# First unit's receptance and key products in fp32 with whole operands, their weights' parts made later, and another order at the start

## The chip, the cores and the metric

The kernel runs on one core of a Trainium2 chip. The metric is device time in microseconds; 660.84 us is the median of three runs before the change (660.57 to 663.16). Engines are named as the profile names them: PE (TensorE), DVE (VectorE), ACT (ScalarE), POOL (GpSimd), SP (the queue that issues the loads and stores).

## The reference

Banded attention over 8 batches, 8 heads and 576 positions of 64 columns (each position sees itself and the 63 before it), then an RWKV channel mix over the 512 joined columns:

```
attn = softmax(q k^T / 8 on the band);  x = (attn v), heads joined: [8, 576, 512]
x_prev = x shifted by one position, zeros first
xk = mu_k*x + (1-mu_k)*x_prev;   xr = mu_r*x + (1-mu_r)*x_prev
k = max(xk @ w_k, 0);   r = 1 / (1 + exp(-(xr @ w_r)))
out = r * ((k*k) @ w_v)
```

The three weights (512x1024, 1024x512, 512x512) arrive as 64-bit floats; q, k, v and mu as fp32.

## The kernel before, in words

The 4608 positions (8 batches of 576) are cut into nine units of 512 (`NU`, `TU`). A unit has four groups, one for each 128 of the 512 columns (two heads). Group by group, a *burst* on PE computes scores (16 fp32 matmuls of 64x128, `bank<-k,q`), transposes exponentials (8 fp32 transposes, `bank<-ident,pr`) and multiplies by the values (16, `bank<-pt,v`). The three parts of a burst belong to three groups that follow each other; only in the first groups they stand apart. DVE masks the scores and takes their least value (`least`, 8 pairs of rows for a group: `pr,nmax<-bank,mask`), ACT takes the exponentials, DVE the reciprocals of the sums, POOL or DVE scales. The result is copied to `xT`, with the column of the position before it.

`mix` then makes xr and xk: ACT or DVE a first term, DVE the blend (`d`). The blended operand is split in two fp32r parts that lie in one tile (`xs`): `high`, a cast on ACT, and `low`, the remainder on POOL or DVE.

A weight comes in chunks of 128x512, 20 in all: numbers 0 to 3 receptance, 4 to 11 key, 12 to 19 value. `decode` turns the 64-bit words into fp32: `sign` (ACT), `clamp` (DVE or POOL, `wt<-wt`), `shift`, `top` and `low` (DVE, the first two into a PSUM bank). `first_part` (a cast on ACT) and `second_part` (the remainder, POOL or DVE) then split the fp32 word into two fp32r parts, tile `ws`.

`product` multiplies: for every 128x128 weight piece three fp32r matmuls of 128x512 (high with high, high with low, low with high) add into one bank. In a unit there are 16 pieces for the receptance product (4 columns by 4 contraction steps), 32 for the key product and 32 for the value product. `r_units` makes the gate from the receptance bank: ACT a tanh and an exponential, DVE a minimum, an and-mask and the last product. `k_units` squares the rectified key and splits it (`ks`). `v_units` multiplies value banks by the gates and stores.

The order is not written down: each step is a `Piece` with a key, a cost and the engines that it may run on, and `play` lays the pieces out with a model of costs, of the rooms in each pool (8 PSUM banks, 14 large tiles `xs`) and of the port that DVE and POOL share. Keys set who goes first: `begin` for bursts, `DECODE` for chunks, `keys` for the mixes. Each engine then runs its pieces in that fixed order and waits where an operand is late. Almost every instruction is recorded by one helper, so the profile gives one line (L69 before, L79 after) for all of them, and tiles tell them apart.

Of the kernel before, what the change touches and what calls it, by code (L numbers as in the profile page):

```python
# [37 lines left out]

STEP = 6
# [3 lines left out]
JOINED = 6  # L43
LINK = 80
# [6 lines left out]
def attn_rwkv_kernel(ctx, tc, qT, kT, v2, mu_k, mu_r, w_k, w_v, w_r, out):  # L51
# [24 lines left out]
    class Hold:  # L76


        def __init__(self, tag):  # L79
            self.tag, self.users = tag, []  # L80

    class Piece:


        def __init__(self, engine, key, cost, fn, needs=(), takes=(), uses=(), lag=LINK, spare=0, port=False, size=0):
            self.costs = engine if isinstance(engine, dict) else {engine: cost}
            self.home = next(iter(self.costs))
            self.engine, self.key, self.fn = None, key, fn
            self.needs = [p for p in needs if p is not None]
            self.takes, self.uses, self.lag, self.spare, self.port, self.size = list(takes), list(uses), lag, spare, port, size  # L90
            for hold in (*self.takes, *self.uses):
                hold.users.append(self)
            self.done = None
            pieces.append(self)

    def play():
# [10 lines left out]
        times = [0]  # L107
        while any(left.values()):
            assert times, [(e, [(p.key, p.fn.__name__) for _, _, p in ps[:4]]) for e, ps in left.items()]
            now = heapq.heappop(times)  # L110
            while ends and ends[0][0] <= now:
                _, _, p = heapq.heappop(ends)
                for hold in (*p.takes, *p.uses):
                    users[id(hold)] -= 1
                    if not users[id(hold)]:
                        room[hold.tag] += 1
            for e, ps in left.items():
                if free[e] > now:
                    continue
                for _, n, p in ps:  # L120
                    if not all(q.done is not None and q.done + (q.lag if q.engine != e else 30) <= now for q in p.needs):
                        continue
                    tags = [h.tag for h in p.takes]
                    if any(room[tag] < tags.count(tag) + (p.spare if tag == "m" else 0) for tag in set(tags)):
# [8 lines left out]
                    for tag in tags:  # L133
                        room[tag] -= 1
# [22 lines left out]

    def pool_ns(n):
        return 195 + 2.1 * n

# [46 lines left out]
    def load_w(count):  # L207

        for n in range(len(raw), len(raw) + count):
            ws, w, i, c = chunks[n]  # L210

            def load(e, w=w, i=i, c=c, n=n):
                raw[n] = const.tile([P, WC, 2], U32, name="w", tag="w", bufs=len(chunks))
# [9 lines left out]
    words = {}  # L223

    def decode(n, loaded):
# [20 lines left out]
        def low(e):  # L246
            dve.scalar_tensor_tensor(words[n].bitcast(U32), raw[n][:, :, 0], 29, words[n, 0],
                                     op0=ALU.logical_shift_right, op1=ALU.bitwise_or)

        def first_part(e):  # L250
            ws[i, c] = const.tile([P, 2, WC], F32R, name="ws", tag="w", bufs=len(chunks))
            sca.copy(ws[i, c][:, 0], words[n])

        def second_part(e):
            engines[e].tensor_sub(ws[i, c][:, 1], words[n], ws[i, c][:, 0].bitcast(F32))

        p = Piece("ACT", key, 600, sign, [loaded], takes=[word])
        p = Piece({"DVE": 430, "POOL": 1000}, key, 0, clamp, [p], port=True)
        p = Piece("DVE", key, 700, shift, [p], takes=bits)
        p = Piece("DVE", key, 700, top, [p])  # L260
        p = Piece("DVE", key, 700, low, [p], uses=bits)
# [104 lines left out]
    def burst(key, gs=None, gt=None, gx=None, halves=(0, 1)):  # L366
        needs, takes, uses, cost, then = [], [], [], 100, []
        if gs is not None:
            needs.append(arrived[gs])
            uses += held[gs]  # L370
            cost += 1030
# [3 lines left out]
        if gx is not None:  # L375
            needs += [arrived["v", gx], *(chain.pop((gx, h, "kept")) for h in range(2))]
            uses += [*held["v", gx], *(chain.pop((gx, h, "pt")) for h in range(2))]
            cost += 1080
# [3 lines left out]
        if gt is not None:  # L382
            for h in halves:
                needs += chain.pop((gt, h, "scaled"))
                uses.append(chain.pop((gt, h, "pr")))
                cost += 355
# [95 lines left out]
    def mix(u, mu, mu1, c, key, after):  # L482
        g = u * NC + c
        state, scratch, x2, hold = [], Hold("tmp"), [], Hold("xs")
        by = []

        def diff(e):
            x2.append(act.tile([P, 2, TU], F32R, name="xs", tag="xs", bufs=SB))
            state.append(tmp.tile([P, TU], F32, name="d", tag="tmp", bufs=TB))
            by.append(e)  # L490
            if e == "ACT":
                sca.activation(state[0], xTs[g][:, :TU], AF.Copy, scale=mu1[:, c:c + 1])
            else:
                dve.tensor_sub(state[0], xTs[g][:, 1:], xTs[g][:, :TU])

        def blend(e):
            x, xp = xTs[g][:, 1:], xTs[g][:, :TU]
            if by[0] == "ACT":
# [13 lines left out]
        def high(e):  # L512
            sca.copy(x2[0][:, 0], state[0])

        def low(e):
            engines[e].tensor_sub(x2[0][:, 1], state[0], x2[0][:, 0].bitcast(F32))

        homes = {"ACT": act_ns(TU) + 90, "DVE": d1(TU)}
        p = after = Piece(homes if u < 2 else dict(reversed(homes.items())), key, 0, diff,
                          [*got[g], after, arrived["mu"]], [scratch, hold], port=True)  # L520
        p = Piece("DVE", key, d1(TU) + 30, blend, [p], uses=[held["x", g]], port=True)
        if 0 < -u * UB % NB < UB:
            p = Piece({"POOL": 200, "ACT": 190}, key, 0, seam, [p], uses=[held["x", g]])
        p = Piece("ACT", key, act_ns(TU), high, [p])
# [18 lines left out]
    def product(key, w, col, x, made, uses, count, n, spare=0):  # L543


        ps, held, last = [], [Hold("bank"), Hold("m")], opened[-1]
        for c in range(count):
            def fn(e, c=c):
                if c == 0:
                    ps.append(bank(TU))  # L550
                for a, b in ((0, 0), (0, 1), (1, 0)):
# [3 lines left out]
            needs = [last, *made[c], *decoded[id(w), c, col * P // WC]]  # L555
            last = Piece("PE", key + 3 * c / STEP, 3 * (13 + n / 2.4), fn, needs,
                         held if c == 0 else [], uses(c), lag=200, spare=spare if c == 0 else 0)
# [4 lines left out]
    def r_units(key, u, xr, gate, n=TU):  # L562
        made, hold = [x[2] for x in xr], [x[1] for x in xr]

        for m in range(NC):
            ps, held, p = product(key, wr_s, m, lambda c, e: xr[c][0][0][:, e], made, lambda c: [hold[c]], NC, n,
                                  spare=u > 0)
            state, scratch, result = [], Hold("tmp"), Hold("r")

            def powers(e, ps=ps, state=state):  # L570
                state += [tmp.tile([P, TU], F32, name="th", tag="tmp", bufs=TB),
                          tmp.tile([P, TU], F32, name="r", bufs=R_BUFS)]
                sca.activation(state[0], ps[0], AF.Tanh, scale=0.5)
                sca.activation(state[1], ps[0], AF.Exp)

            def share(e, state=state):
                th, r = state
                dve.tensor_scalar(r, r, 1.0, None, op0=ALU.min)
# [4 lines left out]
            p = Piece("ACT", key, 2 * act_ns(n), powers, [p], [scratch, result], held)  # L583
            p = Piece("DVE", key, 2 * d2(n) + d1(n), share, [p], uses=[scratch], port=True)
            gate.append((state, result, p))

    def k_units(key, u, xk, k2, n=TU):
        made, hold = [x[2] for x in xk], [x[1] for x in xk]
        for f in range(NF):
            ps, held, p = product(key, wk_s, f, lambda c, e: xk[c][0][0][:, e], made, lambda c: [hold[c]], NC, n,  # L590
                                  spare=u > 0)
            state, scratch, result = [], Hold("tmp"), Hold("xs")

            def relu(e, ps=ps, state=state):
                state.append(tmp.tile([P, TU], F32, name="kf", tag="tmp", bufs=TB))
                sca.activation(state[0], ps[0], AF.Relu)

# [6 lines left out]
            def high(e, state=state):  # L604
                state.append(act.tile([P, 2, TU], F32R, name="ks", tag="xs", bufs=SB))
                sca.copy(state[1][:, 0], state[0])
# [5 lines left out]
            p = Piece("ACT", key, act_ns(n), relu, [p], [scratch], held)  # L612
            p = Piece({"POOL": 150 + 1.8 * n, "ACT": act_ns(n)}, key, 0, square, [p])
            p0 = Piece("ACT", key, act_ns(n), high, [p], [result])
# [4 lines left out]
    def v_units(key, u, k2, gate, n=TU):  # L619
        for m in range(NC):  # L620
            ps, held, p = product(key, wv_s, m, lambda c, e: k2[c][0][1][:, e], [k[2] for k in k2],
                                  lambda c: [k2[c][1]], NF, n, spare=u > 0)
# [17 lines left out]
    DECODE = [-28 + 3 * n for n in range(4)] + [-14 + 2 * n for n in range(8)] + [2 + 2 * n for n in range(8)]  # L640
# [25 lines left out]
    def begin(k):  # L666
        return -30 + k if k < 4 else 10 * k - 60 if k >= JOINED + 2 else (-8, 0, 6, 12)[k - 4]
# [17 lines left out]

    last = None
    for u in range(NU):
# [3 lines left out]
        if u == 0:  # L691
            keys = {"xr": (-24, -23, -22, -21), "xk": (-19, -18, -17, -16)}
        else:
            keys = {"xr": [base - 40 + k for k in (25, 27, 29, 31)], "xk": [base - 40 + k for k in (33, 35, 37, 39)]}
        for nm, mu, mu1 in (("xr", mur, mur1), ("xk", muk, muk1)):
            xs[nm] = []
            for c in range(NC):
                xs[nm].append(mix(u, mu, mu1, c, keys[nm][c], last))
# [38 lines left out]
```

## Time and profile before

| what | value |
|---|---|
| median of three runs | 660.84 us |
| profiled execution: time, span | 662.79 us, 661.0 us |
| granted clock of PE over the span | 0.987 |
| first receptance product (TensorE) | 32.46 us |
| first key product | 58.11 us |
| first value product | 85.04 us |
| score matmuls of group 11 (start) | 143.73 us |

The last row serves as a common point: what lies behind it is the steady part, and both kernels reach it with the same products made. A product of one weight piece shows as three MATMUL rows when it is split. An fp32 matmul shows as two rows for one instruction: the 16 score matmuls of a group are 32 rows.

### The profile page before, as it was taken

To read this page: it belongs to the slowest core of one execution; us is meant where nothing else is said; L and a number is where in the kernel's file an instruction comes from. 1 tells how busy PE (TensorE), PEld (TensorE's weight loads), DVE (VectorE), ACT (ScalarE), POOL (GpSimd) and SP (SyncE) were. 2 spreads that over 40 slices of the span, in tenths; PEclk is the share of its full clock that TensorE was granted. 3 is DMA by queue.
4 is the path that set the end of the run, shared out by engine and by line. 5 is a ranking of instruction groups with operands and counts; after the bars stand their busy time and mean duration, and the time that the engine had idled before them with its cause. 6 is when DMAs were issued, how large, how long until landed. Compare 5 with 4: busy or idle time off the path is not lost.

```text
span 661.0 us, 12919 instructions
## 1 busy us (share of the span) xinstructions
PE 631.5 (96%) x4752; PEld 511.1 (77%) x4752; DVE 409.0 (62%) x1193; ACT 412.8 (62%) x1122; POOL 118.5 (18%) x186
## 2 busy tenths in 40 slices
PE   4875989999999999999999999999999999999997
PEld 4654768778888888888888888888888888888886
DVE  4899987795676467546755675558554766273311
ACT  6878695587754775477646864677367835671540
POOL 5468870110020012001200120001100110000000
PEclk9896999989999999999999999999999999999999
DMA  8991023522132113222332232223322210000001
GB/s 319 401 330 46 2 63 102 153 71 81 55 108 80 56 53 107 79 63 62 95 94 63 62 95 96 69 68 101 98 67 66 98 65 1 1 33 32 1 0 64
DMA packets 47583, 57.87 MB, mean 88 GB/s; under 512 B 7584, under 2 KB 39328, under 8 KB 47520
## 3 DMA queue, kind: packets, MB, share of 16 engines
q1 hardware_dynamic: 47520, 57.04, 26.7%
q8 instruction: 38, 0.62, 0.4%
q14 instruction: 25, 0.20, 0.1%
HBM read 47.58 MB, written 9.44 MB: 86 GB/s over the span
## 4 chain that ended last, share of the span: by engine, by line
PE 87%; DVE 5%; ACT 3%; issue 2%; DMA 1%; SPq 1%; POOL 0%; ACTq 0%; DVEq 0%; POOLq 0%
PE bank L69 87%; DVE bank L69 2%; DVE wt L69 1%; DMA qks<-qT 1%; ACT pr L69 1%; DVE r L69 1%; ACT d L69 1%; SPq L69 1%; ACT kf L69 0%; DVE pr L69 0%; DVE d L69 0%; ACT pt L69 0%; ACT ws L69 0%; ACT wt L69 0%; POOL xs L69 0%
## 5 line engine op out<-in xcount | busy, mean ns | idle before, releaser
L69 PE MATMUL bank<-xs,ws 128*128 128x512 f32 x1296 | 314.4, 398 | 7.1 <-DVE nmax L69 5.7
L69 PEld LDWEIGHTS bank<-xs,ws 128*128 128x128 f32 x1296 | 243.8, 190 | 64.7 <-issue 6.2
L69 PE MATMUL bank<-ks,ws 128*128 128x512 f32 x864 | 209.6, 396 | 1.2 <-ACT kf L69 1.2
L69 PEld LDWEIGHTS bank<-ks,ws 128*128 128x128 f32 x864 | 161.4, 188 | 38.5 <-ACT kf L69 1.9
L69 ACT ACTIVATE pr<-pr,nmax 128x128 f32<-128x128 f32 x288 | 111.8, 393 | 2.5 <-DVE nmax L69 2.3
L69 DVE TENSOR_TENSOR ks<-kf,ks 128x512 fp32r<-128x512 f32 x66 | 46.2, 701 | 83.0 <-ACT ks L69 82.9
L69 ACT ACTIVATE kf<-bank 128x512 f32<-128x512 f32 x72 | 43.0, 598 | 48.6 <-PE bank L69 47.0
L69 ACT COPY xT<-bank 128x512 f32<-128x512 f32 x34 | 20.0, 589 | 79.1 <-PE bank L69 79.0
L69 DVE CUSTOM_DVE_ANT_0 pr<-bank,maskNone 128x128 f32<-128x128 f32 x224 | 53.4, 285 | 14.9 <-PE bank L69 14.9
L69 DVE SCALAR_TENSOR_TENSOR r<-bank,r 128x512 f32<-128x512 f32 x36 | 24.9, 692 | 58.1 <-PE bank L69 58.0
L69 ACT ACTIVATE th<-bank 128x512 f32<-128x512 f32 x36 | 21.5, 598 | 62.7 <-PE bank L69 59.6
L69 POOL TENSOR_TENSOR kf<-kf 128x512 f32<-128x512 f32 x13 | 13.5, 1042 | 248.8 <-ACT kf L69 248.8
L69 ACT ACTIVATION_READ_ACCUMULATOR pr<-pr,nmax 128x1 f32 x288 | 55.1, 191 | 0.0
L69 PE MATMUL bank<-k,q 64*64 64x128 f32 x1088 | 40.8, 286 | 11.2 <-DMA q<-qT 6.5
L69 PEld LDWEIGHTS bank<-k,q 64*64 64x64 f32 x1088 | 31.7, 138 | 23.8 <-issue 9.1
L69 ACT CAST xs<-d 128x512 fp32r<-128x512 f32 x72 | 42.9, 616 | 6.5 <-DVE d L69 4.1
L69 ACT CAST ks<-kf 128x512 fp32r<-128x512 f32 x72 | 44.3, 617 | 1.8
L69 PE MATMUL bank<-ident,pr 128*128 128x128 f32 x288 | 43.1, 292 | 2.0 <-DVE pr L69 1.8
L69 PE MATMUL bank<-pt,v 128*64 128x64 f32 x1120 | 43.0, 229 | 2.0 <-ACT pt L69 2.0
L69 PEld LDWEIGHTS bank<-pt,v 128*64 128x64 f32 x1120 | 37.6, 141 | 9.0 <-issue 5.4
L69 POOL TENSOR_TENSOR xs<-d,xs 128x512 fp32r<-128x512 f32 x14 | 27.8, 1987 | 79.6 <-ACT xs L69 79.6
L69 POOL TENSOR_SCALAR pr<-pr,rs 128x128 f32<-128x128 f32 x68 | 28.5, 441 | 60.9 <-ACT d L69 50.2
(56 smaller groups left out, 580.3 us busy)
## 6 DMA issues: line engine op xcount, KB each, us to landing
v<-v SPq DMA_DIRECT2D x31, 192.0 KB, 2.9
w<-w_k SPq DMA_DIRECT2D x8, 512.0 KB, 8.3
w<-w_v SPq DMA_DIRECT2D x8, 512.0 KB, 10.7
v<-v SPq DMA_DIRECT2D x32, 128.0 KB, 2.4
v<-v SPq DMA_DIRECT2D x15, 256.0 KB, 3.5
v<-v SPq DMA_DIRECT2D x36, 64.0 KB, 2.5
w<-w_r SPq DMA_DIRECT2D x4, 512.0 KB, 5.7
outT<-r SPq DMA_DIRECT2D x8, 256.0 KB, 2.6
```

The source lines that it names most:

```text
L69: return lambda *args, **kw: tc.keep_in_program_order(op(*args, **kw))
```

## The change

- `direct` is true in unit 0 for receptance and key. There the operand is not split: `mix` writes the blend into one half of a shared tile (`xm`), `decode` writes the fp32 word into one half of a shared tile (`whole`), and `product` issues one fp32 matmul (`bank<-xm,whole`) in place of three. The value product and all later units are as before.
- The two parts of the receptance and key weights are still made, for unit 1, with keys of their own (`SPLIT`): chunks with higher numbers come first.
- More steps may run on more engines: the mix's first term and blend on POOL, the casts (`high`, `first_part`) on POOL.
- The gate of unit 0 (`GATES`): ACT takes abs, rectified negative, tanh and exponential (four instructions for two), DVE only the last product (one for three).
- `BEGIN`, `DECODE`, `MIX` and `MIX1` give new keys for the first groups, all chunks and the first two units' mixes. Some costs in the planner differ.

```diff
+GATES = 1
+DIRECT = "rk"
+SPLIT = (28, -13)
+BEGIN = (-31, -29, -29, -22, -9, -7, 14, 20)
+DECODE = (-35, -25, -1, -13, -17, -5, -4, -1, -10, 2, 11, 14, 12, 13, 15, 17, 22, 30, 26, 52)
 ...
         def low(e):
-            dve.scalar_tensor_tensor(words[n].bitcast(U32), raw[n][:, :, 0], 29, words[n, 0],
+            if plain:
+                if pairs[n // 2] is None:
+                    pairs[n // 2] = act.tile([P, 2, WC], F32, name="whole", tag="xs", bufs=SB)
+                words[n, 1] = pairs[n // 2][:, n % 2]
 ...
+        plain = direct(ws, 0)
 ...
+            whole[id(ws), i, c] = p, word, n
+            key = SPLIT[0] + SPLIT[1] * n
 ...
-        p0 = Piece("ACT", key, 560, first_part, [p])
+        p0 = Piece({"ACT": cast_ns(WC), "POOL": pool1_ns(WC)}, key, 0, first_part, [p], port=True)
 ...
+    def direct(ws, u):
+        return u == 0 and any(ws is a and nm in DIRECT for nm, a in (("r", wr_s), ("k", wk_s), ("v", wv_s)))
 ...
+                if plain:
+                    o = col * P % WC
+                    pe.matmul(ps[0], words[whole[id(w), c, col * P // WC][2], 1][:, o:o + P], x(c, None),
+                              start=c == 0, stop=c == count - 1)
+                    return
 ...
+                if u < GATES:
+                    sca.activation(state[0], ps[0], AF.Abs)
+                    sca.activation(state[1], ps[0], AF.Relu, scale=-1.0)
+                    sca.activation(state[0], state[0], AF.Tanh, scale=0.5)
+                    sca.activation(state[1], state[1], AF.Exp, scale=-1.0)
+                    return
```

On PE, around the receptance product and the start of the key product (`xs,ws` are split operand and weight parts, `xm,whole` the unsplit ones), the order was:

```order
L69 MATMUL bank<-pt,v 64x64 x16
L69 MATMUL bank<-ident,pr 128x128 x8
L69 MATMUL bank<-pt,vs 64x64 x16
L69 MATMUL bank<-xs,ws 128x512 x45
L69 MATMUL bank<-k,q 64x128 x16
L69 MATMUL bank<-xs,ws 128x512 x3
L69 MATMUL bank<-k,q 64x128 x16
```

and is now:

```order
L79 MATMUL bank<-pt,v 64x64 x16
L79 MATMUL bank<-xm,whole 128x512 x7
L79 MATMUL bank<-ident,pr 128x128 x4
L79 MATMUL bank<-xm,whole 128x512
L79 MATMUL bank<-ident,pr 128x128 x4
L79 MATMUL bank<-pt,vs 64x64 x16
L79 MATMUL bank<-xm,whole 128x512 x8
L79 MATMUL bank<-k,q 64x128 x16
L79 MATMUL bank<-xm,whole 128x512 x3
L79 MATMUL bank<-k,q 64x128 x16
```

Seven receptance products stand ahead of group 3's transposes and values; group 4's scores come after the whole receptance product, and three key products stand between them and group 5's scores.

On DVE, the key operand's blends of unit 0 (`d<-xT,muk`) stood among the decoding of key chunks, with their remainders behind them:

```order
L69 SCALAR_TENSOR_TENSOR d<-xT,muk,d 128x512
L69 TENSOR_SCALAR wt<-wt 128x512
L69 SCALAR_TENSOR_TENSOR d<-xT,muk,d 128x512
L69 TENSOR_SCALAR bank<-wt 128x512
L69 SCALAR_TENSOR_TENSOR bank<-w,bank 128x512
L69 SCALAR_TENSOR_TENSOR wt<-w,bank 128x512
L69 SCALAR_TENSOR_TENSOR d<-xT,muk,d 128x512
L69 TENSOR_TENSOR xs<-d,xs 128x512
```

They now stand behind six of the eight score rows of group 4 (two rows for each, the second `nmax`):

```order
L79 ISA pr,nmax<-bank,maskNone 128x128
L79 ISA nmax 128x1
L79 SCALAR_TENSOR_TENSOR xm<-xT,muk,xm 128x512
L79 SCALAR_TENSOR_TENSOR xm<-xT,muk,xm 128x512
L79 SCALAR_TENSOR_TENSOR xm<-xT,muk,xm 128x512
L79 SCALAR_TENSOR_TENSOR xm<-xT,muk,xm 128x512
L79 ISA pr,nmax<-bank,maskNone 128x128
```

All four key blends now come together, after group 4's scores, and no remainder follows them.

More of the change, by code (lines that the diff above doesn't have):

```diff
@@ L37 @@
 SB = 14
+GATES = 1
+DIRECT = "rk"
+SPLIT = (28, -13)
+WHOLE = 890
 STEP = 6
@@ L107, in play @@
         times = [0]
+        kept = len({id(h) for p in pieces if p.keeps for h in p.takes})
         while any(left.values()):
@@ L132, in play @@
                         left[o].remove((p.key, n, p))
-                    for tag in tags:
-                        room[tag] -= 1
+                    for hold in p.takes:
+                        if not hold.open:
+                            hold.open = True
+                            kept -= p.keeps
+                            room[hold.tag] -= 1
                     p.engine = e
@@ L250, in first_part @@
         def first_part(e):
-            ws[i, c] = const.tile([P, 2, WC], F32R, name="ws", tag="w", bufs=len(chunks))
-            sca.copy(ws[i, c][:, 0], words[n])
+            ws[i, c] = const.tile([P, 2, WC], F32R, name=f"ws{n}", tag=f"w{n}", bufs=1)
+            copy(e, ws[i, c][:, 0], words[n, 1])
         def second_part(e):
-            engines[e].tensor_sub(ws[i, c][:, 1], words[n], ws[i, c][:, 0].bitcast(F32))
-        p = Piece("ACT", key, 600, sign, [loaded], takes=[word])
-        p = Piece({"DVE": 430, "POOL": 1000}, key, 0, clamp, [p], port=True)
@@ L259, in decode @@
-        p = Piece("DVE", key, 700, shift, [p], takes=bits)
-        p = Piece("DVE", key, 700, top, [p])
-        p = Piece("DVE", key, 700, low, [p], uses=bits)
-        p0 = Piece("ACT", key, 560, first_part, [p])
+            engines[e].tensor_sub(ws[i, c][:, 1], words[n, 1], ws[i, c][:, 0].bitcast(F32))
+        plain = direct(ws, 0)
+        p = Piece("ACT", key, 670, sign, [loaded], takes=[word])
+        p = Piece({"DVE": 430, "POOL": 680}, key, 0, clamp, [p], port=True)
+        p = Piece("DVE", key, 700, shift, [p], takes=bits, uses=[word] if plain else [])
@@ new lines, in decode @@
+        p = Piece("DVE", key, 700, top, [p])
+        if plain:
+            if n % 2 == 0:
+                pairs[n // 2], rooms[n // 2] = None, Hold("xs")
+            word = rooms[n // 2]
+            p = Piece("DVE", key, 700, low, [p], takes=[word], uses=bits)
+            p.keeps = True
+            whole[id(ws), i, c] = p, word, n
+            key = SPLIT[0] + SPLIT[1] * n
+        else:
+            p = Piece("DVE", key, 700, low, [p], uses=bits)
+        p0 = Piece({"ACT": cast_ns(WC), "POOL": pool1_ns(WC)}, key, 0, first_part, [p], port=True)
@@ L366, in burst @@
     def burst(key, gs=None, gt=None, gx=None, halves=(0, 1)):
-        needs, takes, uses, cost, then = [], [], [], 100, []
+        needs, takes, uses, cost, then = [], [], [], 85, []
         if gs is not None:
@@ L370, in burst @@
             uses += held[gs]
-            cost += 1030
+            cost += 1034
             two = banks_of("s", "s")
@@ L385, in burst @@
                 uses.append(chain.pop((gt, h, "pr")))
-                cost += 355
+                cost += 424 if gx is not None else 355
                 own, = banks_of("t")
@@ L497, in blend @@
             x, xp = xTs[g][:, 1:], xTs[g][:, :TU]
-            if by[0] == "ACT":
+            if e == "POOL":
+                part = x2[0][:, 1].bitcast(F32)
+                pool.tensor_scalar(part, *((state[0], mu[:, c:c + 1]) if by[0] == "DVE" else (x, mu[:, c:c + 1])), 1.0,
+                                   op0=ALU.mult, op1=ALU.mult)
+                pool.tensor_add(state[0], xp if by[0] == "DVE" else state[0], part)
+            elif by[0] != "DVE":
                 dve.scalar_tensor_tensor(state[0], x, mu[:, c:c + 1], state[0], op0=ALU.mult, op1=ALU.add)
@@ L541, in attn_rwkv_kernel, with product @@
     opened = [None]
-    def product(key, w, col, x, made, uses, count, n, spare=0):
+    def product(key, w, col, x, made, uses, count, n, spare=0, u=1):
         ps, held, last = [], [Hold("bank"), Hold("m")], opened[-1]
+        plain = direct(w, u)
         for c in range(count):
```

129 lines of the change are left out of this document (90 added, 39 removed).

## The prediction

> **What bounds the kernel now.** I read the page's totals and slices first, then a table of busy time by stretches, then who waited for whom, then TensorE's timeline where the table shows a hole.
>
> ```profile
> span 661.0 us, 12919 instructions
> PE 631.5 (96%) x4752; PEld 511.1 (77%) x4752; DVE 409.0 (62%) x1193; ACT 412.8 (62%) x1122; POOL 118.5 (18%) x186
> PE   4875989999999999999999999999999999999997
> ```
>
> One slice is 16.5 us. PE is full from the tenth slice on; what it lacks lies in the first nine. I cut the span where PE's work changes kind (PE, PEld, DVE, ACT, POOL busy, granted clock):
>
> ```profile
> 0.00:32.46 32.46, 21.82 (x288) 17.68 (x288) 20.65 (x94) 23.87 (x84) 15.76 (x48) 0.95 0.96 359
> 32.46:46.14 13.68, 13.19 (x82) 9.54 (x80) 12.89 (x18) 9.92 (x18) 8.77 (x7) 1.00 0.97 356
> 46.14:58.11 11.97, 2.12 (x32) 1.51 (x33) 11.94 (x42) 10.91 (x34) 8.67 (x8) 0.72 0.45 132
> 58.11:103.60 45.49, 42.74 (x293) 33.73 (x294) 42.36 (x99) 35.95 (x83) 33.21 (x39) 0.96 0.08 24
> 103.60:143.73 40.13, 38.15 (x333) 30.53 (x331) 30.30 (x102) 26.91 (x95) 5.29 (x10) 0.96 0.43 129
> 143.73:640.00 496.27, 496.27 (x3657) 404.55 (x3657) 288.07 (x839) 305.24 (x812) 46.78 (x74) 1.00 0.21 65
> ```
>
> From 143.73 us PE never idles, with DVE busy 58% and ACT 62% (288.07 and 305.24 of 496.27). So the end follows from one number: when PE reaches that point with the work ahead of it done. The worst stretch is the third, where PE works 2.12 of 11.97 us and DVE 11.94.
>
> ```profile
> PE bank L69 <- DVE nmax L69: 5.7, 1, 5.7
> PE bank L69 <- DVE wt L69: 5.2, 3, 4.1
> ```
> ```profile
> 50.77 1.70 PE L69 MATMUL bank<-k,q 64*64 64x128 f32 x30 [4.06 <-DVE wt L69]
> 58.11 1.62 PE L69 MATMUL bank<-xs,ws 128*128 128x512 f32 x3 [5.65 <-DVE nmax L69]
> 60.24 1.54 PE L69 MATMUL bank<-xs,ws 128*128 128x512 f32 x3
> 61.97 15.68 PE L69 MATMUL bank<-xs,ws 128*128 128x512 f32 x66
> ```
>
> The receptance product of the first unit is done at 46.14; the key product begins at 58.11. Between them stands DVE: decoding weights (wt) and the softmax of groups 4 and 5 (nmax). The stage is bound by DVE's queue, not by PE or the loads.
>
> **The change, part by part.** *The dearer product.* One product of a 128x128 weight piece was three fp32r matmuls; for 16 receptance and 32 key pieces of unit 0 it becomes one fp32 matmul, which the trace does not show at this size.
>
> ```profile
> 92.09 8.62 PE L69 MATMUL bank<-ks,ws 128*128 128x512 f32 x36
> 100.64 1.10 PE L69 MATMUL bank<-k,q 64*64 64x128 f32 x32
> 101.67 1.15 PE L69 MATMUL bank<-pt,v 128*64 128x64 f32 x32
> 102.75 1.09 PE L69 MATMUL bank<-ident,pr 128*128 128x128 f32 x8
> 103.60 7.93 PE L69 MATMUL bank<-ks,ws 128*128 128x512 f32 x33
> 634.02 0.85 PE L69 MATMUL bank<-xs,ws 128*128 128x512 f32 x3
> 634.72 0.87 PE L69 MATMUL bank<-ks,ws 128*128 128x512 f32 x3
> ```
>
> Start to start, three fp32r matmuls take 634.72 - 634.02 = 0.70 us. The nearest fp32 rows: four transposes (8 records, full 128x128, 128 columns) take 103.60 - 102.75 = 0.85, or 0.213 per 128 columns, so 0.85 for 512. The score matmuls (four quadrants at a time, 128 columns) take 1.03/4 = 0.26, so 1.03. I take 0.88, near the transposes, which fill the array as the new product does; the bounds are 0.85 and 1.03. The 48 products then cost 48 x (0.88 - 0.70) = +8.6 us of PE, bounds +7.2 and +15.8.
>
> The Trainium skill (FP8 and Floating Point Precision, section TensorE Precision Notes) speaks against the change: true fp32 takes four passes through the array. Priced at a third of a triple each, 0.233, that is an estimate of 0.93 and +11.0 us, between the bounds above.
>
> *The start.* Before, a first operand went blend, cast, remainder on POOL; the last step alone:
>
> ```profile
> 26.57 0.75 DVE L69 SCALAR_TENSOR_TENSOR d<-xT,mur,d 128x512 f32<-128x512 f32 x1 [0.20 <-ACT d L69]
> 28.19 1.81 POOL L69 TENSOR_TENSOR xs<-d,xs 128x512 fp32r<-128x512 f32 x1 [2.67 <-ACT xs L69]
> 28.69 1.97 PE L69 MATMUL bank<-ident,pr 128*128 128x128 f32 x8
> 32.46 3.29 PE L69 MATMUL bank<-xs,ws 128*128 128x512 f32 x13
> ```
>
> Now the blend (27.3) is enough, and the transposes and values of group 3 (28.69 to 32.46) come after seven products. The first product can start near 28.8 instead of 32.46. The second weight chunk and blend must be there soon after, and DVE now splits the first weight chunk between the softmax of groups 0 and 1, some 0.7 us and a wait for ACT's cast, with group 1's score rows queued behind it; I allow 27 to 31. Then 16 x 0.88 = 14.1, group 3's transposes 0.85 and values 1.08: receptance done at 44.8, group 4's scores at 45.8. The 3.7 us won at the start are spent on dearer products: before, it was 46.14.
>
> *The hole.* The first key product waits for DVE's queue. In the changed order DVE has ahead of it 38 score rows, 26 decode instructions (9 shifts, 9 tops, 8 lows), 7 clamps, 6 blends, 3 copies, 4 pairs of share instructions, 1 split and 2 small ones. Durations:
>
> ```profile
> 33.33 0.69 DVE L69 TENSOR_SCALAR bank<-wt 128x512 uint32<-128x512 uint32 x1
> 34.05 0.70 DVE L69 SCALAR_TENSOR_TENSOR bank<-w,bank 128x512 uint32<-128x512 uint32 x1
> 34.79 0.69 DVE L69 SCALAR_TENSOR_TENSOR wt<-w,bank 128x512 uint32<-128x512 uint32 x1
> 51.05 0.28 DVE L69 CUSTOM_DVE_ANT_0 pr<-bank,mask 128x128 f32<-128x128 f32 x1
> 51.26 0.28 DVE L69 CUSTOM_DVE_ANT_0 pr<-bank,maskNone 128x128 f32<-128x128 f32 x1
> 27.84 0.42 DVE L69 TENSOR_SCALAR wt<-wt 128x512 f32<-128x512 f32 x1
> 24.55 0.68 DVE L69 COPY pt<-bank 128x512 f32<-128x512 f32 x1
> 22.07 0.16 DVE L69 TENSOR_SCALAR rs<-sums 128x8 f32<-128x8 f32 x1
> 22.27 0.20 DVE L69 RECIPROCAL rs<-rs 128x8 f32<-128x8 f32 x1
> ```
>
> 38 x 0.21 (start to start) = 8.0; 26 x 0.69 = 17.9; 7 x 0.42 = 2.9; 6 x 0.75 = 4.5; 3 x 0.68 = 2.0; 4 x 0.36 = 1.4; 0.7 + 0.5; in all 37.9 us. Before, DVE had worked 20.65 + 12.89 + 11.94 = 45.5 us by 58.11. What is gone from the queue is group 5's scores, one to two chunks, two key blends and two operand remainders. DVE cannot start before the first scores (6.32), and by 32.46 it had idled 32.46 - 6.32 - 20.65 = 5.5 us for its inputs. With the same idle, 6.3 + 5.5 + 37.9 = 49.7. The other path, group 4's scores at 45.8 plus six score rows and two blends (1.3 + 1.5), gives 48.6. I take 50.5, since DVE's instructions stretch while POOL works:
>
> ```profile
> 40.42 1.76 POOL L69 TENSOR_TENSOR ws<-wt,ws 128x512 fp32r<-128x512 f32 x1
> 40.94 1.53 DVE L69 TENSOR_SCALAR wt<-wt 128x512 f32<-128x512 f32 x1
> 42.38 1.78 DVE L69 SCALAR_TENSOR_TENSOR d<-xT,muk,d 128x512 f32<-128x512 f32 x1
> ```
>
> A clamp of 0.42 took 1.53 and a blend of 0.75 took 1.78 beside POOL's remainders. POOL still makes the parts of the weights in this time, so this stays; bounds for the key product's start are 48.6 and 54.
>
> A hole of about 3 us also costs less behind it: after the old one the first triple took 60.24 - 58.11 less two transposes (0.7), or 1.4 us instead of 0.70, at a granted clock of 0.72. The Trainium skill (TensorE: Matmul & The Clock Gate, section What's actually happening) has the clock halve after an idle window of about 3.4 us; by that rule a 3 us hole may keep it, and the trace agrees as far as it goes: the half-speed triple stands behind a wait of 5.65 us.
>
> *Key product to the common point.* From 50.5: 32 x 0.88 = 28.2; group 5's scores 1.0; group 4's transposes 0.85; bursts 6 and 7 at 103.60 - 100.64 = 2.96 each, 5.9; six value-product records 1.4: 37.4, so 87.9. The decode of the last key chunk has 19.8 us more of DVE queue ahead (16 decode instructions, 10 score rows, 4 gates, 2 blends, copies): ready at 70.3, needed about 72. That is what comes late next; I allow 2 us: 89.9. Before, the same work was done at 103.60 less 39 records of (100.64 - 92.09)/36 = 0.2375, or 94.3. Gain there 4.4.
>
> From there to the start of burst 11:
>
> ```profile
> 133.15 1.02 PE L69 MATMUL bank<-ident,pr 128*128 128x128 f32 x4 [1.84 <-DVE pr L69]
> 143.73 1.10 PE L69 MATMUL bank<-k,q 64*64 64x128 f32 x32
> ```
>
> Before: 143.73 - 94.3 = 49.4. Full speed: 150 records x 0.2375 = 35.6 and three bursts 8.9, 44.5. The stall at 133.15 came from bursts 9 and 10 standing nine records apart; the order now has 36 and more between bursts. I allow 1.1 us: 45.6, so 89.9 + 45.6 = 135.5 against 143.73: -8.2 us.
>
> *What costs nothing.* The parts of key and receptance weights, made later, take 12 casts and 12 remainders; they are hidden behind the fp32 products, but the first split products of unit 1 need them, over 20 us later. The value weights' last parts have 29.6 us of DVE queue behind 70.3, so 100; needed near 113 for the last eighth of the value product. The gates of unit 0 lose two DVE instructions each and gain two on ACT (4 x 2 x 0.6 us); ACT idles in every stretch shown. In later units POOL takes 26 mixes and 21 casts: it worked 46.78 of 496.27 us there. Uncovered, each would add about a microsecond, once per operand. The loads' order on SP is unchanged but for one pair of stores; nothing waits for those.
>
> The sum stands on the profiled execution: 661.0 - 8.2 = 652.8 us span. That run took 662.79 us; the runs' median is 660.84, 1.95 below. Against the median I predict 660.84 - 8.2, **652.6 us**.
>
> **The rivals.** *All cover holds*: no late chunk, products at 0.85, start at 27. That takes off the 2 and 1.1 us allowed and 32 x 0.03 = 1.0: -12.3, and with the key start at 48.6 -14.2: 647. For it: by the queue sums the last key chunk (70.3 against 72) and the value parts (100 against 113) are in time. Against it: no early stretch of the trace is free of stalls.
>
> *The win is eaten*: key product at 54 and the value product waiting some 4 us for parts, since POOL and DVE exclude each other as at 40.42. That adds 3.5 + 4 to -8.2: 660.
>
> *Slower: the hole stays.* Key banks come free only when ACT has read the receptance banks, and ACT's queue now holds four instructions per gate with group 4's eight exponentials between them, which wait for DVE. If DVE is as late as before, the key product starts at 58.1 again; with 37.4 + 2 it ends its stage at 97.5 against 94.3, and with the later stalls as before: +3.2, 664; with products at 1.03 another 4.8, 669. It turns slower once the key product starts later than 58.7 at my price, or 50.5 + 3.4 at 1.03. For it: DVE was 11.94 of 11.97 us busy there. Against it: 7.6 us have left its queue.
>
> **How the numbers follow.** Forecast 0.55, full cover 0.17, win eaten 0.15, hole stays 0.13. Below 0.5% (3.3 us, about what a measurement can tell from no change) lie the forecast, full cover and a fifth of the third: faster 0.75; same 0.12; slower 0.13. The range, 645 to 661.5, takes in full cover and the win eaten, and leaves out the slow case and a little below.
>
> **What would show it.** In the changed profile: 48 products of about 0.88 us; the first before 31 us, the key product at 49 to 52, PE full from about 52 with gaps of 2 us in all; burst 11 near 135.5; the rest as now, about 517 us. It is wrong if a product is over 1 us, if DVE still shows a hole over 6 us before the key product, or if PE idles in the value product or after 140.

## The result, and the profile after

The changed kernel takes 652.44 us (median, 651.96 to 653.41) against 660.75 us for the kernel before on the same chip: a ratio of 0.987, with a 95% interval of 0.985 to 0.989, or 8.3 us less. The profiled execution took 653.41 us with a span of 651.6; the one before took 662.79 with a span of 661.0. That pair differs by 9.4 us.

The page's totals and TensorE's slices (16.3 us each) of the kernel after:

```profile
span 651.6 us, 12842 instructions
...
PE 632.5 (97%) x4704; PEld 497.0 (76%) x4704; DVE 399.6 (61%) x1174; ACT 389.4 (60%) x1076; POOL 144.5 (22%) x250
...
PE   4879999999999999999999999999999999999997
```

From the fourth slice on TensorE's digit is now 9; before, that was so from the seventh, with stalls up to 133 us. PE's busy time hardly moved (631.5 to 632.5): the dearer products fill time in which it waited or ran slowly. POOL has taken 26 us more (118.5 to 144.5), DVE and ACT 33 less together.

The table by stretches of the kernel after, cut at the same times as before up to 143.73 (busy time of PE, PEld, DVE, ACT, POOL, then granted clock, DMA share and GB/s):

```profile
0.00:32.46 32.46, 20.86 (x259) 14.43 (x260) 21.78 (x96) 24.54 (x85) 19.26 (x56) 1.00 0.94 346
32.46:46.14 13.68, 12.76 (x94) 6.67 (x92) 12.61 (x25) 11.32 (x21) 10.55 (x16) 1.00 0.94 350
46.14:58.11 11.97, 9.12 (x44) 4.21 (x45) 8.78 (x40) 8.71 (x33) 5.61 (x11) 0.71 0.47 151
58.11:103.60 45.49, 45.49 (x333) 28.77 (x332) 42.86 (x110) 39.33 (x109) 34.93 (x50) 1.00 0.25 72
103.60:143.73 40.13, 40.13 (x349) 32.63 (x348) 30.22 (x93) 24.29 (x79) 10.34 (x12) 1.00 0.31 95
```

The third stretch was the hole: PE worked 2.12 of 11.97 us there and now works 9.12, though at a granted clock of 0.71. In the two stretches after it PE no longer idles at all (42.74 and 38.15 busy before, now 45.49 and 40.13). TensorE's timeline shows what is left of the hole (start, busy time, what, idle time before it and what ended it):

```profile
27.71 6.27 PE L79 MATMUL bank<-xm,whole 128*128 128x512 f32 x14
...
37.47 7.13 PE L79 MATMUL bank<-xm,whole 128*128 128x512 f32 x16
44.53 1.10 PE L79 MATMUL bank<-k,q 64*64 64x128 f32 x32
48.99 5.46 PE L79 MATMUL bank<-xm,whole 128*128 128x512 f32 x6 [3.36 <-ACT pr L79]
54.38 1.42 PE L79 MATMUL bank<-k,q 64*64 64x128 f32 x32
...
61.00 8.75 PE L79 MATMUL bank<-xm,whole 128*128 128x512 f32 x20
69.68 1.10 PE L79 MATMUL bank<-k,q 64*64 64x128 f32 x32
...
88.87 6.82 PE L79 MATMUL bank<-ks,ws 128*128 128x512 f32 x27
...
137.92 1.10 PE L79 MATMUL bank<-k,q 64*64 64x128 f32 x32
```

An unsplit product is two rows, so `x6` is three products. They take 54.38 - 48.99 = 5.39 us; ten later ones take 69.68 - 61.00 = 8.68, or 0.868 each. So the three products behind the hole ran at half speed. After 48.99 no row of PE up to burst 11 has a wait.

Burst 11 starts at 137.92, but this is not quite the same point as 143.73 before, although the table of the time before calls it a common point: the 96 split records of unit 0's value product stand ahead of it in both orders, but of unit 1 there are 78 now and were 63, so 15 more (of 0.2375 us each). With the same work done, the common point is 137.92 - 15 x 0.2375 = 134.4, so 9.4 us earlier. Behind it lie 517.2 us (before 517.3): all of the profiled pair's gain is made ahead of this point.

| milestone | before | predicted | after |
|---|---|---|---|
| first receptance product | 32.46 | 28.8 | 27.71 |
| first key product | 58.11 | 50.5 | 48.99 |
| key product, bursts 6 and 7 and six value records done | 94.3 | 89.9 | 88.87 |
| common point | 143.73 | 135.5 | 134.4 |
| median | 660.84 | 652.6 | 652.44 |

### The profile page after: what moved, and what is told of

It reads as the page before. It is cut to its first block, busy times and chain, and to the rows that moved or that the text cites. A ratio compares the mean times of both kernels' runs of the same rounds, so it can differ in the third digit from the quotient of the medians.

```text
span 651.6 us, 12842 instructions
## 1 busy us (share of the span) xinstructions
PE 632.5 (97%) x4704; PEld 497.0 (76%) x4704; DVE 399.6 (61%) x1174; ACT 389.4 (60%) x1076; POOL 144.5 (22%) x250
## 4 chain that ended last, share of the span: by engine, by line
PE 94%; ACT 2%; DVE 0%; issue 0%
PE bank L79 94%; ACT pr L79 1%; ACT th L79 0%; ACT pt L79 0%; ACT r L79 0%; ACT xT L79 0%; DVE r L79 0%; ACT xm L79 0%
## 5 line engine op out<-in xcount | busy, mean ns | idle before, releaser
L79 PE MATMUL bank<-xs,ws 128*128 128x512 f32 x1152 | 275.6, 396 | 0.0
L79 PEld LDWEIGHTS bank<-xs,ws 128*128 128x128 f32 x1152 | 215.8, 188 | 49.4
L79 DVE TENSOR_TENSOR ks<-kf,ks 128x512 fp32r<-128x512 f32 x69 | 48.2, 699 | 83.1 <-ACT ks L79 82.5
L79 PE MATMUL bank<-xm,whole 128*128 128x512 f32 x96 | 46.0, 626 | 3.4 <-ACT pr L79 3.4
L79 DVE TENSOR_TENSOR xs<-d,xs 128x512 fp32r<-128x512 f32 x59 | 38.3, 684 | 8.4 <-POOL xs L79 5.6
L79 POOL TENSOR_SCALAR pr<-pr,rs 128x128 f32<-128x128 f32 x88 | 35.4, 424 | 31.0 <-ACT d L79 17.0
L79 PE MATMUL bank<-pt,v 128*64 128x64 f32 x1120 | 41.0, 225 | 1.0 <-ACT pt L79 1.0
L79 PEld LDWEIGHTS bank<-pt,v 128*64 128x64 f32 x1120 | 35.9, 138 | 7.7 <-issue 5.5
L79 ACT CAST xs<-d 128x512 fp32r<-128x512 f32 x57 | 35.4, 620 | 8.6 <-DVE d L79 6.9
```

The source lines that it names most:

```text
L79: return lambda *args, **kw: tc.keep_in_program_order(op(*args, **kw))
```

## The experiments

The first four sections undo one part of the change each. Every run was timed beside runs of the kernel before, whose medians lie between 661.1 and 661.4; the ratio is against those. Only the three runs on the finished order, at the end, leave everything else in its place. In all others the planner lays out the whole start anew, so what such a run measures is its edit together with the order that the planner then makes.

### All products split again

The planner's lists, the choice of engines and the gates stay as after; the diff is in one constant:

```diff
-DIRECT = "rk"
+DIRECT = ""
```

> All products of unit 0 are split again (three fp32r matmuls); the new keys, the flexible engines and the four-instruction gate stay. Theory A (the unsplit products pay by shortening what stands ahead of the key product on DVE, POOL and ACT, and cost 48 x 0.175 = 8.4 us of PE): the key product starts at 54 to 60 us, PE saves 8.4 us later, and the time is 656 to 662 us. Theory B (the new order and the flexible engines bring the gain, the unsplit products only cost PE time): the key product still starts near 49 us and the time falls to 644 to 649 us.

Measured: 666.95 us (666.14 to 668.02), ratio 1.008 [1.006, 1.010]. Neither number: it is slower than the kernel before. TensorE's timeline of this run:

```profile
43.61 0.80 PE L79 MATMUL bank<-xs,ws 128*128 128x512 f32 x1 [2.58 <-POOL ws L79]
...
58.36 2.90 PE L79 MATMUL bank<-ident,pr 128*128 128x128 f32 x8 [5.42 <-POOL pr L79]
60.92 3.28 PE L79 MATMUL bank<-xs,ws 128*128 128x512 f32 x7
```

With split products the early work waits for remainders from POOL (2.58 us within the receptance product), and the hole comes back ahead of group 4's transposes (5.42, booked to POOL's scaling). Against the kernel after, whose lists, engines and gates are the same, unsplit products are worth 666.95 - 652.44 = 14.5 us, although each of the 48 costs PE more. The lists were made for unsplit products; which list would suit split ones best was not tried.

### The old lists

`BEGIN`, `DECODE`, `MIX` and `MIX1` as before (16 receptance and 32 key products stay unsplit, engines and gates stay new):

```diff
-BEGIN = (-31, -29, -29, -22, -9, -7, 14, 20)
+BEGIN = (-30, -29, -28, -27, -8, 0, 6, 12)
-DECODE = (-35, -25, -1, -13, ...)
+DECODE = (-28, -25, -22, -19, ...)
-MIX = ((-51, -31, -47, -56), (-43, -46, -33, -40))
+MIX = ((-24, -23, -22, -21), (-19, -18, -17, -16))
 ...
```

> The keys of before (for the first groups, the chunks and the mixes of units 0 and 1) with the unsplit products kept. Theory A: most of the gain stays, 652 to 657 us, the key product starts before 54 us. Theory B: the gain goes and the dearer products remain, 660 to 669 us.

Measured: 662.44 us (659.63 to 662.95), ratio 1.001 [1.000, 1.002]: B's number, no gain over the kernel before. Its timeline:

```profile
36.77 1.46 PE L79 MATMUL bank<-pt,vs 128*64 128x64 f32 x30 [1.28 <-ACT pt L79]
...
75.11 16.46 PE L79 MATMUL bank<-xm,whole 128*128 128x512 f32 x34 [2.40 <-ACT kf L79]
```

The rest of the change, unsplit products included, brings nothing by itself: the key product does start early, at 51.10, but the waits are only spread out, down to 75.11. The change without the unsplit products (the run above) costs 6 us. Together the two gain 8.3. With these lists, each is good only with the other.

### Only one of the two products unsplit

```diff
-DIRECT = "rk"
+DIRECT = "r"     (the other run: "k")
```

> Only the receptance product is unsplit, the key product is split again. Theory A: PE saves 32 x 0.175 = 5.6 us, but the key parts come before the key product again, so it starts at 53 to 58 us: 653 to 659 us. Theory B: the saving remains, 646 to 649 us.

Measured: 663.17 us (661.32 to 664.94), ratio 1.002 [1.001, 1.004]. The hole of this run, and the one where the key product alone is unsplit, each from TensorE's timeline:

```profile
56.68 1.52 PE L79 MATMUL bank<-ident,pr 128*128 128x128 f32 x4 [7.30 <-POOL pr L79]
```

```profile
51.22 2.10 PE L79 MATMUL bank<-k,q 64*64 64x128 f32 x30 [3.01 <-DVE nmax L79]
```

The key product started at 57.86, as late as before the change, and that is where A had put it (53 to 58); the time is beyond both numbers, since further waits followed (2.24 us at 90.89 for the value operand, 1.41 and 1.65 in unit 1's receptance product).

> The kernel after with the receptance products of the first unit split into parts again and only its key products unsplit; lists of positions and engine choice as after. It completes the square of no unsplit product (666.95), receptance alone (663.17) and both (652.44). If the two halves add up: 666.95 - (663.17 - 652.44) = 656.2, so 655 to 658 us. If the new order needs both (a late receptance stage pushes the rest as in the run with all split, key product not before 53 us): 660 to 665 us.

Measured: 658.32 us (657.09 to 659.79), ratio 0.995 [0.994, 0.997], just above the first number. None 666.95, receptance alone 663.17, key alone 658.32, both 652.44: the halves add up within 2.1 us (3.8 and 8.6 alone, 14.5 together). So neither half needs the other; most of it is the key product's.

### The old choice of engines

POOL may no longer take first terms, blends and casts:

```diff
-        p0 = Piece({"ACT": cast_ns(WC), "POOL": pool1_ns(WC)}, key, 0, first_part, [p], port=True)
+        p0 = Piece("ACT", key, cast_ns(WC), first_part, [p])
-        homes = {"ACT": cast_ns(TU) + 110, "POOL": pool1_ns(TU), "DVE": d1(TU)}
+        homes = {"ACT": cast_ns(TU) + 110, "DVE": d1(TU)}
 ...
```

> The casts run on ACT alone and the mixes' first terms and blends not on POOL, as before; unsplit products and new keys stay. Theory A: 651 to 655 us, since ACT idles in each early stretch and PE is full later. Theory B: 655 to 660 us, since POOL's help is part of what brings the gain. In both the stretch behind 140 us stays at full PE.

Measured: 656.23 us (654.77 to 659.21), ratio 0.992 [0.990, 0.995], by the median B's number. TensorE's timeline has one large wait:

```profile
40.72 5.40 PE L79 MATMUL bank<-xm,whole 128*128 128x512 f32 x8 [4.29 <-DVE xm L79]
```

The last receptance operand then comes 4.29 us late from DVE. POOL's help is worth 3.8 us, by medians, of the gain; the runs spread widely, and the profiled execution (654.93) is only 1.5 us behind that of the kernel after.

### One list at a time

The kernel after with the old `DECODE` alone, then with the old `BEGIN` alone (the diffs are those lines of the run with the old lists).

> The kernel after with the old order of weight decoding alone (the old list of decoding positions; the new positions of the units' starts, the unsplit products and the engine choice stay). If the decoding order carries the gain of the order (the last receptance and key chunks then come late on DVE, and TensorE waits for them): 657 to 663 us, near the 662.4 us with all old lists. If the positions of the units' starts carry it: 652 to 655 us.

> The kernel after with the old positions of the units' starts alone (groups 2 and 3 then begin ahead of the receptance product; the new decoding order, the unsplit products and the engine choice stay). If these positions carry the gain of the order: 657 to 663 us, with the receptance product done near 51 us. If the decoding order carries it: 652 to 655 us.

Measured: 659.38 us (657.57 to 660.43), ratio 0.997 [0.996, 0.998], and 660.85 us (657.03 to 663.33), ratio 1.000 [0.998, 1.002]. Neither list carries the gain alone: each one put back takes nearly all of it. The key product starts at 49.68 and at 52.38, so an early key product alone is not the gain; PE must also have no wait before and behind it. The largest late wait of each, in their timelines:

```profile
74.01 13.98 PE L79 MATMUL bank<-xm,whole 128*128 128x512 f32 x28 [2.54 <-ACT xT L79]
```

```profile
52.38 3.28 PE L79 MATMUL bank<-xm,whole 128*128 128x512 f32 x4 [1.76 <-DVE nmax L79]
```

### Two tries at the hole through the planner

The hole of 3.36 us is where DVE's four key blends stand behind six score rows of group 4:

```profile
46.96 3.22 DVE L79 SCALAR_TENSOR_TENSOR xm<-xT,muk,xm 128x512 f32<-128x512 f32 x4
```

The row is from DVE's timeline of the kernel after. By the durations of the four (one of 1.23 us, three of 0.74) the second ends at 46.96 + 1.23 + 0.74, about 48.9, and the first key product starts at 48.99. The wait is booked to ACT's `pr`, but I read it as a wait for the tile that holds the first two blends. The other candidate, a PSUM bank that ACT has not yet read out, is settled by the last section: there PE writes into this product's own bank from 45.26 on. Two edits let the planner put this work earlier:

```diff
 # first: key mixes of unit 0 not ordered behind the receptance mixes
+                if u == 0 and nm == "xk" and c == 0:
+                    last = None
                 xs[nm].append(mix(u, w, mu, mu1, c, keys[nm][c], last))
 # second: group 4's query and key loads ahead of the value weights
+    load_w(8)
+    load_qk(4)
 ...
```

> The kernel after, with the key blends of the first unit no longer ordered behind the last receptance blend, so that DVE does them before group 4's scores instead of after them. Theory C (what is left early is the hole of 3.36 us behind group 4's scores and the 2.7 us that half the clock costs the three products behind it; the key product then starts at 45.5 to 46): 646 to 650 us. Theory D (DVE's queue is the bound there, the late work only changes its place and the hole goes to group 4's or 5's softmax): 651 to 655 us.

> The kernel after, with group 4's query and key loads issued ahead of the value weights' loads, so that its scores can stand within the receptance product and their rows leave DVE before the key blends. Theory C (hole and half clock go, 6 us): 646 to 650 us. Theory D (DVE's queue is the bound, the hole changes its place): 651 to 655 us.

Measured: 658.03 us (655.77 to 659.35), ratio 0.995 [0.993, 0.997], and 659.37 us (655.1 to 660.09), ratio 0.997 [0.995, 0.998]. Both are 5.6 to 7 us slower than the kernel after, worse than either theory had said. The hole behind group 4's scores is gone, but others came, in the timeline of the first and of the second:

```profile
54.47 1.78 PE L79 MATMUL bank<-xm,whole 128*128 128x512 f32 x2 [2.35 <-DVE whole L79]
...
86.39 2.84 PE L79 MATMUL bank<-xm,whole 128*128 128x512 f32 x6 [1.68 <-ACT kf L79]
```

```profile
47.48 2.08 PE L79 MATMUL bank<-xm,whole 128*128 128x512 f32 x2 [4.79 <-DMA v<-v]
...
104.51 10.15 PE L79 MATMUL bank<-ks,ws 128*128 128x512 f32 x36 [2.33 <-DVE nmax L79]
```

The 4.79 us of the second are booked to a load, but DVE's last receptance blend ends at 47.43 in that run, just ahead of 47.48, so DVE's queue is the likelier cause. Like the runs above, these edits are not clean, since the planner laid out everything anew. So the next runs edit the finished order.

### The hole filled, and the key blends moved, in the finished order

First, 15 products of the identity with a mask, into the first key product's own bank, which that product then overwrites. Nothing else moves:

```diff
+                if c == 0 and u == 0 and w is wk_s and col == 0:
+                    for _ in range(15):
+                        pe.matmul(ps[0][:, :P], ident, masks[None], start=True, stop=True)
```

> The kernel after with every engine's order kept, and 15 fp32 products of the identity with a 128x128 mask (about 0.21 us each) put on TensorE between group 4's scores and the first key product, into that product's own bank, which the product then overwrites: TensorE is busy through the 3.36 us hole, nothing else changes. Theory C (the half clock of the three products behind the hole is real time and follows from the idleness): the clock stays at 1, the three products take 2.65 us instead of 5.39, group 5's scores start at 51.6 instead of 54.38, and 2 to 2.7 us of it reach the end: 649.7 to 651. Theory D (the early stage is DVE's, so that a gain there comes back as a wait in the next 50 us; or the idleness is not what halves the clock): 652 to 653.5 us.

Measured: 650.28 us (649.04 to 651.99), ratio 0.984 [0.982, 0.985] against the kernel before; the profiled execution took 650.0, with a span of 648.2 and a granted clock of 1.0 over that span. TensorE's timeline:

```profile
45.26 3.62 PE L79 MATMUL bank<-maskNone,ident 128*128 128x128 f32 x30
48.71 2.74 PE L79 MATMUL bank<-xm,whole 128*128 128x512 f32 x6
51.38 1.10 PE L79 MATMUL bank<-k,q 64*64 64x128 f32 x32
...
134.52 1.10 PE L79 MATMUL bank<-k,q 64*64 64x128 f32 x32
```

The key product starts no earlier (48.71; the whole run is 0.3 us ahead by then), but its three products take 51.38 - 48.71 = 2.67 us in place of 5.39. Burst 11 comes 3.40 us earlier, and the whole span ends 3.4 earlier, 0.3 of which the run had ahead of the fillers. C holds: the half clock is real time, it follows from the idleness, and nothing behind takes it back. The medians differ by less, 2.2 us, and the two ratios' intervals just touch; the section on the hardware gives a reason. The two kernels were not timed side by side, but every span of this one (647.3 to 649.5) is shorter than every span of the kernel after (650.1 to 651.6).

Second, the four blends on DVE ahead of chunk 7's decoding and of group 4's score rows, by one edit to the finished order:

```diff
-    for p in play():
+    order = list(play())
+    (the four key blends are taken out, and put in front of chunk 7's shift)
+    for p in order:
         p.fn(p.engine)
```

> The kernel after with one edit to the finished order, so that no other choice of the planner changes: the four key blends stand on DVE ahead of the decoding of chunk 7 and of group 4's score rows instead of behind them. The first key product can then start at 45.6, straight behind group 4's scores; group 5's scores wait for DVE's rows of group 4 (about 50.4) instead of standing at 54.38. Theory C (what is left is this hole and its half clock): 2.5 to 4 us less, 648.5 to 650 us. Theory D (DVE's queue is the bound, the late rows and chunks bring the hole back further on): 651 to 654 us.

Measured: 653.18 us (652.25 to 653.37), ratio 0.988 [0.986, 0.989]: no gain, D's number. The timelines of TensorE and of DVE:

```profile
46.02 2.84 PE L79 MATMUL bank<-xm,whole 128*128 128x512 f32 x6
...
51.21 0.43 PE L79 MATMUL bank<-k,q 64*64 64x128 f32 x2 [2.35 <-ACT r L79]
...
61.02 8.75 PE L79 MATMUL bank<-xm,whole 128*128 128x512 f32 x20
```

```profile
44.63 4.75 DVE L79 SCALAR_TENSOR_TENSOR xm<-xT,muk,xm 128x512 f32<-128x512 f32 x4
```

The key product starts straight behind the scores, at 46.02, but group 5's scores wait, and at 61.02 the run is where the kernel after is (61.00). It had been 0.46 us behind at group 4's scores (44.99 for 44.53), and that is all that it won. The blends took 4.75 us here (3.22 in the kernel after), with POOL busy through them, and group 4's rows came behind them, from 50.62 on instead of 45.69. The new hole of 2.35 us also brings the half clock back: the three key products from 53.45 on take 4.20 us.

> Both edits of the two runs beside it: key blends first on DVE, and the 15 filling products ahead of the first key product (the hole that they were made for is then gone, so that they delay the key product by up to 3.2 us). Theory C: no better than the key blends first alone, and up to 3.2 us worse where the key product is what the stage waits for: 649 to 652. Theory D (DVE's rows are awaited anyway, the fillers cover that wait): equal to the key blends first alone within 1 us.

Measured, with both edits: 654.61 us (652.84 to 656.27), ratio 0.991 [0.989, 0.992], 1.4 us above the key blends alone, so neither number quite. The timeline of the profiled execution, which was the fastest of the five, has one wait left:

```profile
56.88 1.37 PE L79 MATMUL bank<-ident,pr 128*128 128x128 f32 x4 [1.64 <-POOL pr L79]
```

The fillers keep the clock in this execution (0.999; the other four show 0.997), and what decides then is group 4's softmax: its transposes start at 56.88 where the filled kernel has them at 55.09. So, of these four versions, the best has the score rows ahead of the key blends, as the changed order has them, and the hole filled, not moved.

## Why the prediction was right

The time (652.6 predicted, 652.44 measured) and the forecast's mechanism hold: the key product starts some 9 us earlier, and PE does not lose it later. The second half of that is as needed as the first, as the runs with old lists show. That the sum came out within 0.2 us is partly luck, since terms that were off cancelled. By the steps:

- **The dearer product: right.** 0.88 was taken; the timeline gives 0.868 for ten in a row and (44.53 - 37.47)/8 = 0.8825 for the last eight of the receptance product, so 48 x 0.17 = 8.2 us of PE. The estimate of 0.93 by the Trainium skill's four passes (FP8 and Floating Point Precision, section TensorE Precision Notes) was too high here.
- **The start: right.** First product 27.71 (28.8 predicted, 27 to 31), group 4's scores at 44.53 (44.8 predicted).
- **The hole: right in kind, 1.5 us better.** By 48.99 DVE had worked 17.70 + 15.21 + 4.34 = 37.3 us, where 37.9 was counted from the order. Its idle time from its first row (6.35) on was 48.99 - 6.35 - 37.3 = 5.3 us, close to the 5.5 taken over from before. The 0.8 us added for DVE's stretching beside POOL were not needed, though the stretch is there (one blend of 1.23 us among three of 0.74).

```profile
0.00:27.71 27.71, 16.11 (x249) 12.24 (x249) 17.70 (x87) 19.79 (x77) 15.62 (x49) 1.00 0.93 334
27.71:44.53 16.82, 16.41 (x74) 8.00 (x73) 15.21 (x27) 14.46 (x27) 12.59 (x20) 1.00 0.98 380
44.53:48.99 4.46, 1.10 (x33) 0.89 (x33) 4.34 (x17) 4.46 (x16) 3.12 (x5) 0.92 0.84 253
```

- **"A hole of about 3 us also costs less behind it": wrong.** The hole was 3.36 us, and the half clock behind it cost as much again: 2.72 us in the three key products and 0.32 in group 5's scores. The sum gave it no price. The filled hole showed that it is real. The profile before could have warned: its wait of 1.84 us at 133.15, which the prediction shows, is followed by a step at half clock (the section on the hardware has the rows), so a wait need not be long.
- **The late key chunk, 2 us: not there.** The chunk left DVE at 72.47 (the row below, of DVE's timeline); its first product, the 20th, came second in the run that starts at 72.72, about 73.6. The margin was 1.1 us, where 70.3 against 72 had been predicted.

```profile
71.78 0.69 DVE L79 SCALAR_TENSOR_TENSOR whole<-raw,bank 128x512 uint32<-128x512 uint32 x1
```

- **From there to the common point: right, by two errors that cancel.** 134.4 - 88.9 = 45.5 against 45.6 predicted. The prediction counted 150 split records; the timeline before has 153 (90 of the value product, 63 of unit 1), which makes 45.2 at full speed and not 44.5. The 1.1 us allowed for a stall were hardly used: no row waits there.
- **The sum.** 1.5 (key start), 2 (chunk) and 0.1 (later) better, 3.0 (clock) worse, 0.5 of small terms better: 134.4 for 135.5. The common point gained 9.4, not 8.2, and these are the 9.4 of the profiled pair. The medians' 8.3 agrees with the 8.2 predicted, but the changed kernel's profiled run stands 1.0 above its median and the one before 1.95 above its own, so a common point read from one execution is good to about a microsecond.
- **"What costs nothing": half right.** The parts of weights that are made later cost nothing, since PE waits for none of them. POOL's share was booked as free of cost; it is in truth worth 3.8 us, which the sum held without naming, as the queue was counted from an order in which POOL had already taken that work.
- **The rivals.** *The hole stays* is what happens to half the change: with receptance alone unsplit the key product starts at 57.86, and 663.17 follows. *The win is eaten* (about 660) is the time that each list put back gives, though not by its mechanism: the key product starts at 49.68 and 52.38 there, not at 54. *All cover holds* (647) came true in its cover, with no late chunk and the key product at 48.99; what it lacks is mainly the clock's share, and the filled kernel's 650.28 is still 3 us above it.

## What to carry to other kernels

Price an edit of arithmetic together with the order that it allows: here the change without its new order gained nothing, without its dearer products it lost 6 us, and whole it gained 8.3: 48 products that are 0.17 us dearer free two engines from work that stood in the way of the first results. Where a short hole ahead of TensorE's main work can't be closed, work that is thrown away can hold the clock through it, and that can be had without moving anything else. An early start for one operand is no gain if the engine that makes it is the one that the next group's chain waits for.

## What the runs showed of the hardware that was not expected

**The granted clock falls for holes of under 2 us, and stays down for whole steps of 3.41 us.** The stretches below are cut at the times at which the granted clock changes, or at whole steps from there; the first fence is the kernel before, the second the kernel after, the third the one with the old `BEGIN`.

```profile
47.88:51.29 3.41, 0.53 (x17) 0.53 (x21) 3.41 (x16) 3.26 (x10) 3.26 (x3) 1.00 0.57 173
51.29:54.70 3.41, 1.17 (x24) 0.77 (x13) 3.41 (x14) 3.41 (x15) 3.31 (x4) 0.50 0.26 62
54.70:58.11 3.41, 0.00 (x0) 0.03 (x1) 3.38 (x13) 2.61 (x10) 2.10 (x3) 0.50 0.36 102
58.11:61.53 3.42, 3.42 (x10) 2.76 (x11) 3.42 (x13) 3.42 (x13) 3.36 (x9) 0.50 0.00 0
61.53:64.94 3.41, 3.41 (x18) 2.79 (x17) 2.89 (x7) 2.95 (x8) 2.60 (x3) 1.00 0.00 0
...
129.80:133.21 3.41, 1.43 (x29) 1.11 (x26) 3.04 (x6) 3.41 (x9) 0.00 (x0) 1.00 0.51 148
133.21:136.62 3.41, 3.41 (x10) 2.70 (x11) 3.41 (x10) 3.03 (x7) 1.54 (x1) 0.50 0.75 216
```

```profile
44.84:48.25 3.41, 0.79 (x32) 0.55 (x21) 3.29 (x16) 3.41 (x12) 2.81 (x4) 1.00 0.80 231
48.25:51.66 3.41, 2.67 (x3) 1.17 (x4) 3.41 (x9) 2.38 (x11) 0.00 (x0) 0.50 0.85 276
51.66:55.08 3.42, 3.42 (x17) 1.37 (x18) 1.01 (x4) 2.31 (x5) 3.05 (x7) 0.50 0.05 17
55.08:58.49 3.41, 3.41 (x33) 1.75 (x28) 2.60 (x18) 2.08 (x10) 1.05 (x3) 1.00 0.35 97
```

```profile
42.61:46.02 3.41, 1.80 (x35) 1.00 (x34) 3.34 (x5) 1.94 (x3) 3.32 (x5) 1.00 0.84 218
...
49.44:52.85 3.41, 1.65 (x34) 1.16 (x34) 3.41 (x21) 2.06 (x11) 0.56 (x1) 1.00 0.85 238
52.85:56.26 3.41, 3.41 (x7) 1.22 (x5) 3.38 (x17) 3.41 (x11) 1.43 (x4) 0.50 0.43 143
```

Behind the hole ahead of the key product the clock was at half for three steps before, two after, one with the old `BEGIN`. In that last run PE had worked 1.65 us of the step, so a hole of 1.76 us was enough; an earlier hole of the same run, of 1.61 us at 45.88, left the clock at 1, with PE at work for 1.80 us of its step. So it is the share of the step that counts rather than the length of one hole. Cut into such steps, the fourteen traces agree from 40 us on: PE worked 1.65 us or less in each step ahead of a fall, and 1.72 or more in every other at full clock. Earlier, where much of the work is narrow or transposes, the clock fell behind busier steps too (24.0 to 27.4 us of the kernel before, with 2.4 us busy). In the kernel after, a step in which PE worked 2.67 of 3.41 us did not bring the full clock back; the next one, wholly busy, did. The Trainium skill (TensorE: Matmul & The Clock Gate, section What's actually happening) names a free-running window of 3413 ns; the steps agree with it, but a whole idle window is not needed: in the second fence 0.79 us of work in the step did not keep the clock, nor did 1.65 in the third.

The steps do not start with the kernel: the falls at 51.29, 48.25 and 52.85 of the three traces lie no whole steps apart. So the price can vary from run to run of one kernel: two steps are 2 x 3.41 x 0.5 / 651.6 = 0.5% of the mean clock, and the profiled execution after shows 0.995, while the other runs of the kernel after show 0.997, which would be one step. That fits a gain of 3.4 us against the profiled execution and of 2.2 by medians for filling the hole; those other runs have no trace. With the old `BEGIN`, runs show 1.000, 0.997 or 0.994. One caution: up to about 17 us the profile gives 1.00, but the rows run at half speed there (32 score records take 1.99 us at 4.20 in the kernel after, and 1.10 from 20.27 on).

What stays open: why the new order with all products split is slower than the old one is known only as far as its waits (for POOL's remainders and scaling). The gates' new form, the later making of the weights' parts (`SPLIT`) and the mixes' lists were not run apart from the rest.
